# One core, attention and two feed-forward layers: the weight conversions' integer addition moves to VectorE, three attention units take P times V in plain float32, and the norms of phi are made by two operations

## The chip, the core and the metric

The kernel runs on one core of a Trainium2 chip. A core has engines that work side by side, each through its own queue, in order: TensorE (PE in the profile, with PEld for its weight loads), VectorE (DVE), ScalarE (ACT), GpSimd (POOL) and SyncE (SP, which here only issues transfers). The metric is the device time of one execution in microseconds (us).

## The reference, cut to what matters

```
scores = q k^T / 8, causal;  a = softmax(scores)              # B 4, H 8, S 576, D 64
local  = a v
phi(x) = where(x > 0, x, exp(x) - 1) + 1
mem    = (phi(q) M) / (phi(q) . z + 1e-6)
attn   = sigmoid(beta) * mem + (1 - sigmoid(beta)) * local    # as 2304 x 512
h      = attn @ w_in1;  g = s * relu(h)^2 + b;  x = g @ w_out1      # 512 -> 2048 -> 512
h      = x @ w_in2;     g = h * tanh(softplus(h));  out = g @ w_out2
```

The four weight matrices arrive as 64-bit floats, and the kernel makes 32-bit floats of them itself.

## The kernel before

**Stages.** Three run into one another: attention, the first layer (`first`, `y_part`: matmuls at L798 and L871), the second layer (matmuls at L1003 and L1069). Beside the first stage the weights of layer 1 are converted in 32 pieces of 128x512 (`convert(1, ...)`), and beside the last third of layer 1 those of layer 2, in 32 more.

**The order.** Nearly every operation is a step with an engine, an estimated duration and a priority. `Plan.order` plays the steps through and writes each engine's queue in the order that comes out; on the chip each engine then runs its queue in that order, and waits on semaphores. While PE has nothing to do in the first 85 us of that plan, it gets products of zeros (L1239).

**Attention.** A unit is one batch and head. It has five tiles of 128 queries, group TA (tiles 0 to 2) and group TB (tiles 3 and 4). Batch 0 runs as eight TA half-units and then eight TB half-units, called `early`; batches 1 to 3 are 24 whole units. Of a unit: phi of q (L498 on POOL, L499 on ACT, L500 on DVE); the norms phi . z, one 64-wide product with a running sum for each tile, which is an operation and a read of its accumulator (L492), then L496 and L504; the memory columns of P (L555, POOL); scores (L534 for an early unit, L538 and L539 for the others); masked row minimum (L543); exp (L552); scaling of each tile's rows (L569 on POOL or DVE, L567 on ACT, by the letters of `E_NORM` and `F_NORM`); transposes (L596); P times V (L624); copy to `xs` (L632) and out.

In a unit that isn't early the products are split: each operand is a rounded high part and a low rest, both in a faster matmul format. So P's transposes are copied high by ACT (L601) and subtracted to a low part by DVE (L604), V likewise (L646, L647), each matmul of P times V runs once with `PTh` and once with `PTl`, and DVE adds the two halves of the result (L635). An early unit takes P times V in plain float32, without a low part and without L604, L646, L647 and L635.

**A conversion** (`convert`): a transfer brings 512 pairs of words; ACT scales the high word into the new exponent (L695) and rounds the low word to its top three bits (L700); DVE shifts the first by three (L702) and puts the sign in (L703); POOL adds the two as integers (L705); for layer 1 ACT then makes the high part (L712) and DVE the low rest (L715).

Of the kernel before, what the change touches and what calls it, by code (L numbers as in the profile page):

```python
# [9 lines left out]
F32 = mybir.dt.float32  # L10
F32R = mybir.dt.float32r
BF16 = mybir.dt.bfloat16
I32 = mybir.dt.int32
U32 = mybir.dt.uint32
AF = mybir.ActivationFunctionType
ALU = mybir.AluOpType
PSUM = bass.MemoryType.PSUM
DRAM = bass.MemoryType.DRAM

P = 128  # L20
MASKED = -1.0e30
HUGE = 3.0e38
SIGN = -0x80000000
PE, ACT, DVE, POOL, DMA = range(5)


# [8 lines left out]
CONV = (3.0, 3.81, 4.18, 3.12)  # L35
CONV2 = 655.2

E_TRA, E_NORM, E_XS = 'AAAADA', 'PPDDA', 'A'
F_NORM = 'PPDDA'
C_HI, C_W, C2_W = 'AAAA', 'AAAA', 'AAAA'  # L40

PLACE_A = (0, 3, 2, 4)
# [289 lines left out]
def attention_then_two_ffn(ctx: ExitStack, tc: tile.TileContext, qk, qz, vm, beta,  # L332
# [99 lines left out]
    def unit(b, h, prio, groups=(TA, TB), place=None):  # L432
# [5 lines left out]
            attention_steps.append(plan.add(engine, us, prio, f, r, w, keep=keep, share=share))  # L438

        early = place is not None and place < 5  # L440
        first_half = groups == (TA,)
        tiles = [t for g in groups for t in g]
        nb = tiles[-1] + 1
# [44 lines left out]
            return qn()[:, lo_t + 1:lo_t + n_t + 1]  # L488

        def norm_phi():  # L490
            for t in tiles:
                nc.vector.tensor_tensor_reduce(qn()[:, t + 1, :], ex.t[:, t, :], qn()[:, 0, :], 1.0, 0.0,  # L492
                                               ALU.mult, ALU.add, nm.t[:, t:t + 1])

        def norm_gate():
            nc.vector.tensor_scalar(nm.t[:, mine], nm.t[:, mine], 1e-6, igate[:, 0, h:h + 1], op0=ALU.add, op1=ALU.mult)  # L496
# [2 lines left out]
        add(ACT, act_us(n_t * D), lambda: nc.scalar.activation(ex.t[:, mine], ex.t[:, mine], AF.Exp), [ex], [ex])  # L499
        add(DVE, dve_us(n_t * D), lambda: nc.vector.scalar_tensor_tensor(ex.t[:, mine], q_rows(), 0.0, ex.t[:, mine],  # L500
                                                                         op0=ALU.max, op1=ALU.add), [ex, qn_b], [ex])
        add(DVE, 0.22 * n_t, norm_phi, [ex, qn_b], [nm, qn_b])
        add(DVE, 0.13, norm_gate, [nm], [nm])
        add(DVE, 0.09, lambda: nc.vector.reciprocal(nm.t[:, mine], nm.t[:, mine]), [nm], [nm])  # L504

# [75 lines left out]
        def weigh(g):  # L581


            first = {t: 2 * t if t < 3 else 4 * (t - 3) for t in g}
            names = ("PTh", "PTl") if not early else (("PTl",) if h % 2 else ("PTh",))
            PT = [Buf(R[x], [P, 9, P], F32 if early else F32R) for x in names]
            for t in g:
                cuts = (0, t + 1) if t < 4 else (0, 3, 5)
                for c0, c1 in zip(cuts, cuts[1:]):
                    ps = Buf(R["a"], [P, 4, P])  # L590
                    at_ = slice(first[t] + c0, first[t] + c1)
                    n = c1 - c0

                    def mm(ps=ps, t=t, c0=c0, c1=c1):
                        for c in range(c0, c1):
                            nc.tensor.transpose(ps.t[:, c - c0, :], Pt[t].t[:, c * P:(c + 1) * P], ident)  # L596

                    e = on(E_TRA[t + (c0 > 0)]) if early else ACT

                    def high(ps=ps, at_=at_, n=n, dve=e == DVE):  # L600
                        (nc.vector.tensor_copy if dve else nc.scalar.copy)(PT[0].t[:, at_], ps.t[:, :n])  # L601

                    def low(ps=ps, at_=at_, n=n):
                        nc.vector.tensor_tensor(PT[1].t[:, at_], ps.t[:, :n], PT[0].t[:, at_].bitcast(F32), op=ALU.subtract)  # L604

                    add(PE, 0.01 + 0.108 * n, mm, [Pt[t]], [ps], PT)
                    add(e, dve_us(n * P) if e == DVE else act_us(n * P) - 0.04, high, [ps], [PT[0]])
                    if not early:
                        add(DVE, dve_us(n * P), low, [ps, PT[0]], [PT[1]])

            n = len(g) * P
            skip = D if g[0] == 0 else 0
            m = n - skip
            q0 = max(0, g[0] * P - D)
            pv, xs = Buf(R["a"], [P, 512]), Buf(R["xs"], [D, 320])

            def mm():
                for c in range(g[-1] + 1):
                    ts = [t for t in g if t >= c]
                    f = [first[t] + c for t in ts]  # L620
                    cols = slice((ts[0] - g[0]) * P, n)
                    for k, x in enumerate(PT):
                        o, v = (pv.t[:D, cols], vx()[:, c, :]) if early else (pv.t[:, cols], V.t[:, c, :])
                        nc.tensor.matmul(o.rearrange("p (t q) -> p t q", q=P), v,  # L624
                                         x.t[:, f[0]:f[-1] + 1:f[1] - f[0] if len(f) > 1 else 1, :],
                                         start=(c == 0 and k == 0), stop=(c == g[-1] and k == len(PT) - 1))

            cols = 6 if g == TA else 9
            add(PE, cols * P * 0.0017 if early else 0.06 + cols * P * 0.00085, mm, PT + [vx_b if early else V], [pv])
            e = on(E_XS) if early else ACT  # L630
            add(e, dve_us(m) if e == DVE else act_us(m) - 0.04,
                lambda: (nc.vector.tensor_copy if e == DVE else nc.scalar.copy)(xs.t[:, :m], pv.t[:D, skip:n] if early else pv.t[D:, skip:n]),  # L632
                [pv], [xs])
            if not early:
                add(DVE, dve_us(m), lambda: nc.vector.tensor_tensor(xs.t[:, :m], pv.t[:D, skip:n], xs.t[:, :m], op=ALU.add),  # L635
                    [pv, xs], [xs])
            c0, p0 = b * S + q0, h % 2 * D
            add(DMA, 0.5, lambda: nc.sync.dma_start(x_d[p0:p0 + D, h // 2, c0:c0 + m], xs.t[:, :m]), [xs], [x_in[b, groups_all.index(g)]])
# [2 lines left out]
            score(t)  # L641
        norm(groups[0])
        add(DMA, 0.6 * nb / NQ, lambda: nc.sync.dma_start(vx(), vm[b, h][:, :nb]), w=[vx_b])
        if not early:
            V = Buf(R["V"], [P, NQ, 2 * D], F32R)
            add(ACT, act_us(NQ * D), lambda: nc.scalar.copy(V.t[:, :, :D], vx()), [vx_b], [V])  # L646
            add(DVE, dve_us(NQ * D), lambda: nc.vector.tensor_tensor(V.t[:, :, D:], vx(), V.t[:, :, :D].bitcast(F32), op=ALU.subtract),  # L647
                [vx_b, V], [V])
# [25 lines left out]
    def convert(layer, prio, which, r, j, raw, after=()):  # L674


        w_in, w_out = ((w_in1, w_out1), (w_in2, w_out2))[layer - 1]
        fc = r * FPR + j
        src = w_in[j * P:(j + 1) * P, r * 512:(r + 1) * 512] if which == "in" else w_out[fc * P:(fc + 1) * P, :]
        w = Buf(R["w32"], [P, 512], I32)  # L680

        def words():
            return raw.t[:, :1024].rearrange("p (n two) -> p n two", two=2)

        def f32():
            return w.t.bitcast(F32)

        add(DMA, 1.5, prio, lambda: nc.sync.dma_start(words(), src.bitcast(I32).rearrange("p (n two) -> p n two", two=2)),
            w=[raw], after=after).lag = 1.0 if layer == 1 else 3.0

        e = on((C_W if layer == 1 else C2_W)[j])
        add(e, 0.52 if e == ACT else 0.335, prio,
            (lambda: nc.scalar.activation(f32(), words()[:, :, 1].bitcast(F32), AF.Copy, scale=2.0 ** -112)) if e == ACT else  # L695
            (lambda: nc.vector.tensor_scalar(f32(), words()[:, :, 1].bitcast(F32), 2.0 ** -112, None, op0=ALU.mult)),
            [raw], [w])

        low_words = Buf()
        add(ACT, 0.52, prio, lambda: nc.scalar.activation(words()[:, :, 0], words()[:, :, 0].bitcast(U32), AF.Copy,  # L700
                                                          scale=2.0 ** -29), [raw], [low_words])
        add(DVE, 0.335, prio, lambda: nc.vector.tensor_scalar(w.t, w.t, 3, None, op0=ALU.logical_shift_left), [w], [w])  # L702
        add(DVE, 0.6, prio, lambda: nc.vector.scalar_tensor_tensor(w.t, words()[:, :, 1], SIGN, w.t,  # L703
                                                                   op0=ALU.bitwise_and, op1=ALU.bitwise_or), [raw, w], [w])
        add(POOL, 1.23 if layer == 1 else 1.45, prio, lambda: nc.gpsimd.tensor_tensor(w.t, w.t, words()[:, :, 0], op=ALU.add),  # L705
            [raw, low_words, w], [w])
        if layer == 1:
            hi, lo = f"w{which[0]}h", f"w{which[0]}l"
            hi_dve, lo_dve = C_HI[j] == "D", C_LO[j] == "D"
            half = Buf()  # L710
            add(DVE if hi_dve else ACT, 0.335 if hi_dve else 0.52, prio,
                lambda: (nc.vector.tensor_copy if hi_dve else nc.scalar.copy)(w_at(hi, r, j), f32()), [w],  # L712
                [W[hi, r], half])
            add(DVE if lo_dve else POOL, 0.6 if lo_dve else 1.23, prio,
                lambda: (nc.vector if lo_dve else nc.gpsimd).tensor_tensor(w_at(lo, r, j), f32(),  # L715
                                                                           w_at(hi, r, j).bitcast(F32), op=ALU.subtract),
                [w, half], [W[lo, r]])
        return w
# [568 lines left out]
```

## Time and profile before

| | us |
|---|---|
| median of 3 runs (1041.0 to 1042.43) | 1041.44 |
| the profiled execution | 1041.25 |
| its span on the core | 1039.4 |
| PE busy | 1004.7 (97%) |
| DVE busy | 845.4 (81%) |
| ACT busy | 713.2 (69%) |
| POOL busy | 278.2 (27%) |
| mean granted clock of PE, as a share of full speed | 0.991 |

The span is the time from the core's first to its last instruction, and 1.85 us lie outside it. Shares are means over stages with different limits, and matmuls are pipelined, so PE's busy time counts gaps between matmuls that a reader has to find otherwise.

### The profile page before, as it was taken

The numbers are of one execution on the slowest core, as the hardware profiler recorded it, in microseconds if no ns is written. First come the engines' busy times: TensorE is split into PE (matmuls) and PEld (weight loads), VectorE is DVE, ScalarE is ACT, GpSimd is POOL, SyncE is SP. The second block draws the span as 40 slices with busy tenths as digits, with TensorE's granted clock in tenths as the row PEclk, the third lists the DMA queues.
The fourth block names the chain that finished last, engine by engine and source line by source line (L and its number), as shares of the span: only waits on it lengthen the run. The fifth ranks groups of instructions, "written<-read, shape, count | busy, mean of one in ns | idle before, by whom it ended". The sixth has DMA issues, their size and how long they took to land.

```text
span 1039.4 us, 20180 instructions
## 1 busy us (share of the span) xinstructions
PE 1004.7 (97%) x6708; PEld 928.9 (89%) x6708; DVE 845.4 (81%) x2347; ACT 713.2 (69%) x1606; POOL 278.2 (27%) x386
## 2 busy tenths in 40 slices
PE   6889997999999999999999999999999999999998
PEld 4657787999999999999888778899999999999998
DVE  6899899999999989986568896359985789767864
ACT  6876897888988888876777897536753456434552
POOL 6864354333343334320234220000110000100010
PEclk9998998999999999999999999999999999999999
DMA  9663563323432333225888887558686766676464
GB/s 260 181 195 103 152 193 95 111 85 99 137 111 72 93 119 94 83 64 157 234 254 265 271 290 232 213 192 288 214 295 226 233 220 202 238 236 216 151 218 168
DMA packets 88984, 188.63 MB, mean 181 GB/s; under 512 B 8752, under 2 KB 63024, under 8 KB 81584
## 3 DMA queue, kind: packets, MB, share of 16 engines
q1 hardware_dynamic: 81392, 135.95, 42.3%
q0 software_dynamic: 7056, 51.38, 14.7%
q8 instruction: 53, 0.87, 0.3%
q14 instruction: 51, 0.42, 0.1%
q10 hardware_dynamic: 432, 0.01, 0.0%
HBM read 144.32 MB, written 42.99 MB: 180 GB/s over the span
## 4 chain that ended last, share of the span: by engine, by line
PE 59%; DVE 14%; issue 11%; ACT 7%; DMA 4%; POOL 3%; POOLq 0%; DVEq 0%; ACTq 0%; SPq 0%
PE bank L1003 15%; PE bank L1069 12%; PE bank L871 12%; PE bank L798 11%; PE bank L624 3%; PE bank L596 3%; DVE PTl L604 2%; PE bank L538 1%; DVE Pt L543 1%; PE bank L539 1%; DVE stage L703 1%; ACT PTh L601 1%; ACT Pt L552 1%; DVE stage L702 1%; POOL stage L705 1%
## 5 line engine op out<-in xcount | busy, mean ns | idle before, releaser
L1069 PE MATMUL bank<-woh,S 128*128 128x256 f32 x792 | 107.3, 283 | 0.0
L1069 PEld LDWEIGHTS bank<-woh,S 128*128 128x128 f32 x792 | 100.8, 192 | 0.1
L1069 PE MATMUL bank<-wol,S 128*128 128x256 f32 x720 | 98.1, 283 | 0.0
L555 POOL TENSOR_SCALAR Pt<-ex,nm 128x64 f32<-128x64 f32 x148 | 74.5, 516 | 85.1 <-PE bank L596 38.5
L1003 PE MATMUL bank<-wi,woh 128*128 128x384 f32 x426 | 94.0, 335 | 0.0
L552 ACT ACTIVATE Pt<-Pt,mx 128x64 f32<-128x64 f32 (+4 forms) x148 | 81.8, 555 | 16.5 <-DVE mx L543 15.7
L1069 PEld LDWEIGHTS bank<-wol,S 128*128 128x128 f32 x720 | 91.8, 192 | 0.0
L596 PE MATMUL bank<-ident,Pt 128*128 128x128 f32 x432 | 67.0, 281 | 10.8 <-POOL Pt L569 7.9
L1003 PEld LDWEIGHTS bank<-wi,woh 128*128 128x128 f32 x426 | 75.6, 188 | 0.6
L1003 PE MATMUL bank<-wi,wol 128*128 128x384 f32 x294 | 76.0, 335 | 0.1
L705 POOL TENSOR_TENSOR stage<-stage 128x512 int32<-128x512 int32 x36 | 48.5, 1348 | 99.6 <-DVE stage L703 50.0
L604 DVE TENSOR_TENSOR PTl<-bank,PTh 128x128 fp32r<-128x128 f32 (+1 forms) x144 | 63.8, 480 | 2.3 <-ACT PTh L601 1.2
L596 PEld LDWEIGHTS bank<-ident,Pt 128*128 128x128 f32 x432 | 49.7, 143 | 17.0 <-POOL Pt L569 10.3
L569 POOL TENSOR_SCALAR Pt<-Pt,rs 128x64 f32<-128x64 f32 x64 | 45.3, 749 | 70.7 <-DVE rs L574 54.6
L984 POOL DMA_DIRECT2D wol<-wo_split_d x17 | 9.2, 542 | 201.7 <-DVE wi L727 109.9
L543 DVE CUSTOM_DVE_ANT_0 Pt<-bank,mask 128x320 f32<-128x320 f32 (+3 forms) x148 | 59.1, 416 | 3.3 <-PE bank L539 1.6
L601 ACT CAST PTh<-bank 128x128 fp32r<-128x128 f32 (+1 forms) x144 | 54.8, 430 | 2.6 <-PE bank L596 1.7
L871 PE MATMUL bank<-gh,wol 128*128 128x256 f32 x320 | 54.0, 292 | 0.0
L871 PE MATMUL bank<-gl,woh 128*128 128x256 f32 x320 | 53.7, 290 | 0.0
L1003 PEld LDWEIGHTS bank<-wi,wol 128*128 128x128 f32 x294 | 53.0, 188 | 0.6 <-DMA wol<-wi_split_d 0.3
L871 PE MATMUL bank<-gh,woh 128*128 128x256 f32 x320 | 53.1, 289 | 0.0
L798 PE MATMUL bank<-xh,wi 128*128 128x256 f32 x320 | 50.6, 289 | 1.4 <-DVE rt L849 1.3
(278 smaller groups left out, 2961.9 us busy)
## 6 DMA issues: line engine op xcount, KB each, us to landing
wol<-wo_split_d POOLq DMA_DIRECT2D x17, 1024.0 KB, 5.2
woh<-wo_split_d POOLq DMA_DIRECT2D x16, 1024.0 KB, 5.8
qk<-in_qk SPq DMA_DIRECT2D x24, 608.0 KB, 3.9
stage<-in_w_out SPq DMA_DIRECT2D x23, 512.0 KB, 4.5
wo_split_d<-high SPq DMA_DIRECT2D x44, 256.0 KB, 3.1
stage<-in_w_in SPq DMA_DIRECT2D x21, 512.0 KB, 4.8
stage<-wi_d SPq DMA_DIRECT2D x24, 384.0 KB, 5.3
wi_split_d<-woh SPq DMA_DIRECT2D x8, 1024.0 KB, 4.9
```

The lines of the kernel that those rows point to most:

```text
L543: nc.vector.tensor_tensor_reduce(Pt[t].t[:, D + lo:D + hi], ps.t[:, :hi - lo], mask[:, SP - w + lo:SP - w + hi], -SCALE, mx.t[:, t:t + 1] ...
L552: nc.scalar.activation(Pt[t].t[:, D:w + D], Pt[t].t[:, D:w + D], AF.Exp, bias=mx.t[:, t + i:t + i + 1], scale=-1.0, accum_out=rs.t[:, t:t ...
L555: add(POOL, 0.3, lambda: nc.gpsimd.tensor_scalar(Pt[t].t[:, :D], ex.t[:, t, :], nm.t[:, t:t + 1], 1.0, op0=ALU.mult, op1=ALU.mult), [ex, n ...
L569: (nc.vector if e == DVE else nc.gpsimd).tensor_scalar(x, x, r, None, op0=ALU.mult)
L596: nc.tensor.transpose(ps.t[:, c - c0, :], Pt[t].t[:, c * P:(c + 1) * P], ident)
L601: (nc.vector.tensor_copy if dve else nc.scalar.copy)(PT[0].t[:, at_], ps.t[:, :n])
L604: nc.vector.tensor_tensor(PT[1].t[:, at_], ps.t[:, :n], PT[0].t[:, at_].bitcast(F32), op=ALU.subtract)
L705: add(POOL, 1.23 if layer == 1 else 1.45, prio, lambda: nc.gpsimd.tensor_tensor(w.t, w.t, words()[:, :, 0], op=ALU.add), [raw, low_words, ...
L798: nc.tensor.matmul(ph, w_at(nm, r, cc)[:, o:o + P], x_at(x, cc), start=(part == 0 and cc == 0), stop=(part == 2 and cc == NCC - 1))
L871: nc.tensor.matmul(acc[ec // per].t[:, (ec % per) * n:(ec % per + 1) * n], w_at(nm, r, jj)[:, ec * P:(ec + 1) * P], t(x), start=(big and f ...
L1003: nc.tensor.matmul(ps.t[:, :H2], w[i // 4].t[:, j, kk, i % 4], x[kk].t[:, k], start=begin and part == kk == 0, stop=part == 2 and kk == 1, ...
L1069: nc.tensor.matmul(acc[t].t[:, :DH], s.t[:, j, t * P:(t + 1) * P], x.t[:, k, q % 4], start=q == part == 0, stop=q == NQ2 - 1 and part == 2)
```

## The change

**The conversions.** DVE's operation that put the sign in (128x512 int32) becomes a bit operation on 16-bit halves: the sign bit of the high word goes into the upper half of the low word. DVE then adds the two as integers; the program issues it as one instruction on 1024 16-bit halves. POOL has no part in a conversion any more. The sign's step now waits for ACT's rounding of the low word (L700), since it writes beside it.

**Early units.** Tile 2's rows are scaled by POOL, not by DVE (`E_NORM`), in the eight TA half-units.

**Plain.** The first three units of batch 1 take P times V as early units do (`PLAIN`).

**Norms of phi.** One product over all tiles of the unit, with z broadcast, and one sum over the last axis.

```diff
-E_TRA, E_NORM, E_XS = 'AAAADA', 'PPDDA', 'A'
+E_TRA, E_NORM, E_XS = 'AAAADA', 'PPPDA', 'A'
 F_NORM = 'PPDDA'
+PLAIN = 3
...
         early = place is not None and place < 5
+        plain = early or (b == 1 and h < PLAIN)
...
         def norm_phi():
-            for t in tiles:
-                nc.vector.tensor_tensor_reduce(qn()[:, t + 1, :], ex.t[:, t, :], qn()[:, 0, :], 1.0, 0.0,
-                                               ALU.mult, ALU.add, nm.t[:, t:t + 1])
+            nc.vector.tensor_tensor(q_rows(), ex.t[:, mine], qn()[:, 0:1, :].to_broadcast([P, n_t, D]), op=ALU.mult)
+            nc.vector.tensor_reduce(nm.t[:, mine], q_rows(), axis=AXIS, op=ALU.add)
...
-            names = ("PTh", "PTl") if not early else (("PTl",) if h % 2 else ("PTh",))
-            PT = [Buf(R[x], [P, 9, P], F32 if early else F32R) for x in names]
+            names = ("PTh", "PTl") if not plain else ("PTl" if (h % 2 if early else g == TB) else "PTh",)
+            PT = [Buf(R[x], [P, 9, P], F32 if plain else F32R) for x in names]
...
-                    if not early:
+                    if not plain:
                         add(DVE, dve_us(n * P), low, [ps, PT[0]], [PT[1]])
...
+        def limbs():
+            return raw.t[:, :1024].bitcast(U16).rearrange("p (n four) -> p n four", four=4)
...
-        add(DVE, 0.6, prio, lambda: nc.vector.scalar_tensor_tensor(w.t, words()[:, :, 1], SIGN, w.t,
-                                                                   op0=ALU.bitwise_and, op1=ALU.bitwise_or), [raw, w], [w])
-        add(POOL, 1.23 if layer == 1 else 1.45, prio, lambda: nc.gpsimd.tensor_tensor(w.t, w.t, words()[:, :, 0], op=ALU.add),
-            [raw, low_words, w], [w])
+        signed = Buf()
+        add(DVE, 0.335, prio, lambda: nc.vector.tensor_scalar(limbs()[:, :, 1], limbs()[:, :, 3], 0x8000, None, op0=ALU.bitwise_and),
+            [raw, low_words], [signed])
+        add(DVE, 0.75, prio, lambda: nc.vector.tensor_tensor(w.t, w.t, words()[:, :, 0], op=ALU.add), [raw, signed, w], [w])
```

In the other places of `weigh` and at V's split, `early` becomes `plain` in the same way, and the estimates that `Plan` takes for the changed steps change with them. Line numbers of the changed kernel are two to five higher (L702 becomes L707, L703's place is L709, L705's is L711, L492 becomes L494 and L495, L569 becomes L571, L624 becomes L626).

The plan writes all queues anew. POOL's queue from its first memory columns (L555) on, before: `Pt_0`, `Pt_1` and `B` hold tiles of P.

```order
L555 TENSOR_SCALAR Pt_0_158<-ex_139,nm_149 128x64
L555 TENSOR_SCALAR Pt_0_162<-ex_139,nm_149 128x64
L555 TENSOR_SCALAR Pt_0_174<-ex_139,nm_149 128x64
L498 TENSOR_SCALAR ex_182<-wol_0_134 128x192
L705 TENSOR_TENSOR stage<-stage 128x512
L498 TENSOR_SCALAR ex_209<-woh_0_141 128x192
L569 TENSOR_SCALAR Pt_0_158<-Pt_0_158,rs_160 128x64
L569 TENSOR_SCALAR Pt_0_162<-Pt_0_162,rs_160 128x192
L555 TENSOR_SCALAR Pt_1_215<-ex_182,nm_199 128x64
```

And now:

```order
L557 TENSOR_SCALAR Pt_0_155<-ex_139,nm_149 128x64
L557 TENSOR_SCALAR Pt_0_161<-ex_139,nm_149 128x64
L557 TENSOR_SCALAR Pt_0_170<-ex_139,nm_149 128x64
L500 TENSOR_SCALAR ex_178<-wol_0_134 128x192
L500 TENSOR_SCALAR ex_208<-woh_0_141 128x192
L571 TENSOR_SCALAR Pt_0_155<-Pt_0_155,rs_157 128x64
L571 TENSOR_SCALAR Pt_0_161<-Pt_0_161,rs_157 128x192
L571 TENSOR_SCALAR Pt_0_170<-Pt_0_170,rs_157 128x320
L557 TENSOR_SCALAR Pt_1_215<-ex_178,nm_204 128x64
```

The integer addition is gone from between the units, and a third scaling, 320 wide, has come into each.

DVE's queue at the first conversion, before (`ISA` at L543 is the row minimum and the read of its accumulator, `stage` holds the piece):

```order
L702 TENSOR_SCALAR stage<-stage 128x512
L543 ISA Pt_0_162,mx_159<-bank_111,mask 128x192
L543 ISA mx_159 128x1
L703 SCALAR_TENSOR_TENSOR stage<-stage 128x512
L543 ISA Pt_0_174,mx_159<-bank_112,mask 128x320
L543 ISA mx_159 128x1
L500 SCALAR_TENSOR_TENSOR ex_182<-wol_0_134,ex_182 128x192
```

And now:

```order
L707 TENSOR_SCALAR stage<-stage 128x512
L545 ISA Pt_0_161,mx_156<-bank_111,mask 128x192
L545 ISA mx_156 128x1
L709 TENSOR_SCALAR stage<-stage 128x512
L545 ISA Pt_0_170,mx_156<-bank_112,mask 128x320
L545 ISA mx_156 128x1
L711 ISA stage<-stage 128x1024
```

The sign's operation is a different one in the same place, and the addition, `ISA` on 1024 halves, stands behind it in the same queue.

PE's queue at the first whole unit's P times V, group TA, before (`V` holds V's two parts, the L798 and L871 rows are layer 1):

```order
L871 MATMUL bank_109<-gl_1660,woh_0_1325 128x256 x2
L624 MATMUL bank_113<-PTh_1798,V_1771 128x384
L624 MATMUL bank_113<-PTl_1799,V_1771 128x384
L624 MATMUL bank_113<-PTh_1798,V_1771 128x256
L624 MATMUL bank_113<-PTl_1799,V_1771 128x256
L624 MATMUL bank_113<-PTh_1798,V_1771 128x128
L624 MATMUL bank_113<-PTl_1799,V_1771 128x128
L798 MATMUL bank_106<-xh_890,wih_0_1549 128x256 x4
```

And now (`vx` is V as it was loaded):

```order
L876 MATMUL bank_109<-gh_1748,wol_0_1346 128x256 x2
L626 MATMUL bank_112<-PTh_1889,vx_1777 64x384
L626 MATMUL bank_112<-PTh_1889,vx_1777 64x256
L626 MATMUL bank_112<-PTh_1889,vx_1777 64x128
L598 MATMUL bank_113<-ident,Pt_0_1797 128x128 x4
L598 MATMUL bank_111<-ident,Pt_0_1803 128x128 x3
```

Three plain float32 matmuls stand for six split ones, and the transposes of TB follow them at once. Each plain one shows as two records in a trace.

## Rows read from the trace of the kernel before

**Rows 1.** Windows view: length, busy us and count (PE, PEld, DVE, ACT, POOL), clock, DMA.

```profile
25.00:50.00 25.00, 21.49 (x122) 15.01 (x121) 21.24 (x85) 20.69 (x62) 22.17 (x31) 1.00 0.70 195
...
60.00:200.00 140.00, 126.81 (x824) 106.85 (x823) 130.05 (x398) 110.95 (x263) 59.99 (x74) 0.95 0.47 143
200.00:475.00 275.00, 271.34 (x2165) 263.34 (x2166) 254.63 (x974) 224.00 (x596) 97.29 (x161) 1.00 0.31 93
475.00:650.00 175.00, 172.81 (x843) 145.53 (x843) 132.59 (x249) 138.15 (x264) 45.77 (x32) 0.99 0.82 252
```

**Rows 2.** Chain that ended last, 60 to 200: start, us, what.

```profile
70.23 1.67 DVE stage L703
...
92.29 1.68 DVE wil L715
...
123.40 1.20 DVE rs L572
```

**Rows 3.** Timeline: first and last DVE instruction held beside a POOL addition.

```profile
10.06 1.29 POOL L705 TENSOR_TENSOR stage<-stage 128x512 int32<-128x512 int32 x1 [0.48 <-ACT Pt L552]
...
10.25 1.32 DVE L500 SCALAR_TENSOR_TENSOR ex<-wol,ex 128x192 f32<-128x192 f32 x1
...
29.38 0.34 DVE L500 SCALAR_TENSOR_TENSOR ex<-wih,ex 128x192 f32<-128x192 f32 x1
...
615.62 1.80 DVE L853 TENSOR_TENSOR xh<-g,xh 128x512 fp32r<-128x512 f32 x1
```

**Rows 4.** Windows view of L705 alone (POOL busy us and count, clock, DMA).

```profile
60.00:200.00 140.00, 28.93 (x22) 0.95 0.47 143
```

**Rows 5.** Groups, conversions and norms: count, busy us, mean ns, idle before.

```profile
L703 DVE SCALAR_TENSOR_TENSOR low<-stage,low 128x512 int32<-128x512 int32 x8 | 5.5, 690 | 0.2
L705 POOL TENSOR_TENSOR stage<-stage 128x512 int32<-128x512 int32 x36 | 48.5, 1348 | 99.6 <-DVE stage L703 50.0 <-ACT xs L632 8.6 <-ACT stage L700 5.3
L727 DVE TENSOR_TENSOR woh<-stage,woh 128x1024 fp32r<-128x1024 f32 x14 | 17.1, 1218 | 4.0 <-ACT woh L726 4.0
L492 DVE CUSTOM_DVE_ANT_0 qn<-ex,qn 128x64 f32<-128x64 f32 x136 | 25.5, 241 | 0.6
L492 DVE DVE_READ_ACCUMULATOR2_ANT nm<- 128x1 f32 x160 | 12.4, 78 | 0.0
```

**Rows 6.** Timeline: the shift of a conversion, undisturbed.

```profile
563.01 0.42 DVE L702 TENSOR_SCALAR stage<-stage 128x512 int32<-128x512 int32 x1
```

**Rows 7.** Groups of DVE work that a plain unit leaves out.

```profile
L604 DVE TENSOR_TENSOR PTl<-bank,PTh 128x128 fp32r<-128x128 f32 (+1 forms) x144 | 63.8, 480 | 2.3 <-ACT PTh L601 1.2
L635 DVE TENSOR_TENSOR xs<-bank,xs 64x320 f32<-64x320 f32 (+1 forms) x48 | 21.4, 445 | 4.6 <-ACT xs L632 3.9
L647 DVE TENSOR_TENSOR V<-vx,V 128x320 fp32r<-128x320 f32 x24 | 12.0, 498 | 0.3 <-ACT V L646 0.2
```

**Rows 8.** Timeline: plain TA, then a split TA's first and last matmul.

```profile
34.15 1.51 PE L624 MATMUL bank<-PTl,vx 128*64 128x384 f32 x6
155.32 0.34 PE L624 MATMUL bank<-PTh,V 128*128 128x384 f32 x1
...
156.17 0.28 PE L624 MATMUL bank<-PTl,V 128*128 128x128 f32 x1
```

**Rows 9.** Chain: a plain TB's P times V, an early unit's scores, a split TB.

```profile
112.52 2.09 PE bank L624 x10
...
117.19 2.68 PE bank L534 x8
...
164.96 1.15 PE bank L624 x10
```

**Rows 10.** POOL's group of the 320-wide shape; timeline of POOL and DVE without an addition.

```profile
L498 POOL TENSOR_SCALAR ex<-qn 128x320 f32<-128x320 f32 x24 | 26.2, 1092 | 45.0 <-DMA qn<-in_qz 41.2 <-DVE Pt L569 3.9
...
52.07 3.52 POOL L569 TENSOR_SCALAR Pt<-Pt,rs 128x64 f32<-128x64 f32 x4
...
53.65 0.38 DVE L569 TENSOR_SCALAR B<-B,rs 128x320 f32<-128x320 f32 x1
```

More of the change, by code (lines that the diff above doesn't have):

```diff
@@ L14 @@
 U32 = mybir.dt.uint32
+U16 = mybir.dt.uint16
 AF = mybir.ActivationFunctionType
 ALU = mybir.AluOpType
+AXIS = mybir.AxisListType.X
 PSUM = bass.MemoryType.PSUM
@@ L22 @@
 HUGE = 3.0e38
-SIGN = -0x80000000
 PE, ACT, DVE, POOL, DMA = range(5)
@@ L501, in unit @@
                                                                          op0=ALU.max, op1=ALU.add), [ex, qn_b], [ex])
-        add(DVE, 0.22 * n_t, norm_phi, [ex, qn_b], [nm, qn_b])
+        add(DVE, 2 * dve_us(n_t * D), norm_phi, [ex, qn_b], [nm, qn_b])
         add(DVE, 0.13, norm_gate, [nm], [nm])
@@ L596, in mm @@
                             nc.tensor.transpose(ps.t[:, c - c0, :], Pt[t].t[:, c * P:(c + 1) * P], ident)
-                    e = on(E_TRA[t + (c0 > 0)]) if early else ACT
+                    e = on(E_TRA[t + (c0 > 0)]) if plain else ACT
                     def high(ps=ps, at_=at_, n=n, dve=e == DVE):
@@ L622, in mm @@
                     for k, x in enumerate(PT):
-                        o, v = (pv.t[:D, cols], vx()[:, c, :]) if early else (pv.t[:, cols], V.t[:, c, :])
+                        o, v = (pv.t[:D, cols], vx()[:, c, :]) if plain else (pv.t[:, cols], V.t[:, c, :])
                         nc.tensor.matmul(o.rearrange("p (t q) -> p t q", q=P), v,
@@ L628, in weigh @@
             cols = 6 if g == TA else 9
-            add(PE, cols * P * 0.0017 if early else 0.06 + cols * P * 0.00085, mm, PT + [vx_b if early else V], [pv])
-            e = on(E_XS) if early else ACT
+            add(PE, cols * P * 0.0017 if plain else 0.06 + cols * P * 0.00085, mm, PT + [vx_b if plain else V], [pv], share=0.5 if plain else 1.0)
+            e = on(E_XS) if plain else ACT
             add(e, dve_us(m) if e == DVE else act_us(m) - 0.04,
-                lambda: (nc.vector.tensor_copy if e == DVE else nc.scalar.copy)(xs.t[:, :m], pv.t[:D, skip:n] if early else pv.t[D:, skip:n]),
+                lambda: (nc.vector.tensor_copy if e == DVE else nc.scalar.copy)(xs.t[:, :m], pv.t[:D, skip:n] if plain else pv.t[D:, skip:n]),
                 [pv], [xs])
-            if not early:
+            if not plain:
                 add(DVE, dve_us(m), lambda: nc.vector.tensor_tensor(xs.t[:, :m], pv.t[:D, skip:n], xs.t[:, :m], op=ALU.add),
@@ L643, in unit @@
         add(DMA, 0.6 * nb / NQ, lambda: nc.sync.dma_start(vx(), vm[b, h][:, :nb]), w=[vx_b])
-        if not early:
+        if not plain:
             V = Buf(R["V"], [P, NQ, 2 * D], F32R)
```

## The prediction

> **What bounds the kernel now.** I read the windows view first, since the shares of the page mix stages. From 200 on PE is the limit: 2165 matmul records in 275 us, 7.87 in a microsecond, while DVE is busy for 93% beside it; from 475 to 650 PE is idle for only 2.2 us of 175; and the rest to the end has no stall of PE that is worth a row. Between 60 and 200 it is different: 824 records in 140 us, 5.9 in a microsecond, with DVE busy for 130.05 us (93%) and a granted clock of 0.95 [rows 1]. PE's own need there: 824 records at 7.87 are 105 us. The eight TB half-units take P times V in plain float32, 2.09 us where a split one takes 1.15, so 8 x 0.94 = 7.5 us more; their scores, 48 such records, take 2.68 us for eight where the steady rate gives 1.02, so 10 us more [rows 1, 9]. That makes 122 us, and about 18 us of PE are lost between 60 and 200. [...]
>
> The chain of waits says on what. It runs through DVE instructions far longer than their kind: 1.67 us for the sign, 1.68 for a low rest, 1.20 for a 3-wide operation [rows 2]. Beside each of them POOL adds integers. So I went through DVE's timeline beside all 64 additions and took, for each DVE instruction, what it lasts beyond the lower fifth of its form. Beside 52 of the 64 one lasts clearly longer (over 0.06 us); the first and the last are shown, and the first has 0.34 us without an addition beside it [rows 3]. The excess is 24.5 us beside the first 32 additions, of which 17 us fall between 60 and 200 (22 additions [rows 4]), and 19.3 us beside the 32 of layer 2.
>
> Before 60 the stage of the TA half-units is POOL's: 22.17 of 25 us between 25 and 50 [rows 1].
>
> **Conversions.** A piece loses 1.35 us on POOL [rows 5]. On DVE the sign's 0.69 goes [rows 5], and a bit operation with one input and the integer addition come. For the first the nearest rows are the shift, the same shape with one input, 0.42, and the sign itself, 0.69 [rows 5, 6]; I take 0.42. The trace has no addition on halves: one 512-wide operation with two inputs takes 0.69, a 1024-wide one 1.22 [rows 5]. The instruction has 1024 halves, but 512 words; I take 0.69 and keep 1.22 for the range. So DVE pays 0.42 + 0.69 - 0.69 = 0.42 a piece (at worst 1.22), 9.2 us for 22 pieces, and gets back the 17 us for which the additions held it. The new wait on the rounding of the low word (L700) blocks DVE's queue if ACT is late; ACT makes it right behind L695, for which DVE waits already, so I cost it at nothing: the shift and, in the first piece, a row minimum stand between. If that cover goes, what stands behind it is the next unit's row minimum, and exp on ACT waits for that.
>
> **Plain units.** DVE leaves out six subtractions, 63.8 / 24 = 2.66 us, V's rest, 0.50, and the sum of the halves, 21.4 / 24 = 0.89 [rows 7]: 4.05 a unit, 12.1 in all, all of it before 200, where the split P times V of those three units now begin at 155 and later [rows 8]. PE pays: plain TA 1.51 us against 155.32 to 156.45, 1.13; plain TB 2.09 against 1.15 [rows 8, 9]. That is 0.38 + 0.94 = 1.3 a unit, 4 us.
>
> **Norms.** Five products with their reads are 5 x (0.241 + 0.078) = 1.6 us [rows 5]. In their place stand a product and a sum over 320 elements. No sum over an axis is in the trace; I take the 320-wide two-input 0.50 [rows 7] for both, so 0.6 less for a whole unit, for some five of them before 200: 3 us. If the sum took twice as much, 0.1 would be left. A TA half-unit saves 0.3 (three products, 0.96, against two of the 0.34 of a 192-wide one [rows 3]), a TB one nothing. After 200 the 19 units save 11 us of DVE, which I cost at nothing: PE is full there.
>
> **Tile 2.** Eight scalings leave DVE, 0.38 each, and cost POOL about 1.1, by its other one-input operation of this shape [rows 10]: 8.8 us, against the 10 x 1.35 = 13.5 that it loses before 60. POOL is relieved by 5 us, but each tile 2 comes 0.7 later to its transposes. I take 2 us of gain before 60, with bounds of 5 us either way.
>
> [...] Beside four scalings on POOL, 3.52 us in a row, DVE's own scaling takes 0.38 as ever [rows 10]. [...]
>
> **The sum.** Between 60 and 200 DVE gets 17 - 9.2 + 12.1 + 3 = 23 us less work, from 130 to 107, and PE 4 more, 126. Then PE needs more than DVE, and the 18 us lost are the most that can come back. Some will stay: weights arrive in chains of six steps, and ACT is at 79%. I take two thirds, 12, less the 4: 8 us. Before 60: 2. From 475 to 650 DVE gets 19.3 back and pays 32 x 0.42 = 13.4; PE was idle for 2.2 there: 1. In all 11: 1041.25 - 11 = **1030 us**. The profiled execution lies 0.2 under the median, so this holds for the median too.
>
> **Rivals.**
>
> *The first stage grows.* The eight scalings hold DVE for 24.5 / 31 = 0.8 each, 6 us, in the stage that POOL sets, instead of giving back 2. What speaks for it: tile 2 is the last and the longest of a half-unit. Against: rows 10. 1030 + 8 = 1038.
>
> *The addition is slow.* At 1.22, and 0.69 for the sign, DVE pays 0.8 more a piece, 18 us between 60 and 200, and is relieved by 5 us only. With 2 or 3 of PE's loss back after the 4, and nothing more after 475: 1038.
>
> *PE is the limit already (slower).* If the 18 us are order and clock rather than waits for DVE, the relief buys nothing and the three plain units are paid in full: 1041 + 4 = 1045. It decides if, between 145 and 200, PE's rate stays under 6.5 records a microsecond although DVE has idle time. [...] Against: DVE's 93% and the chain through the held instructions.
>
> *More comes back.* All 18 return, POOL's 5 before 60 and 4 from 475 on: 1041 - 18 + 4 - 5 - 4 = 1018.
>
> **Chances.** Forecast 0.55; first stage 0.12; slow addition 0.13; PE 0.10; more 0.10. The range from 1018 to 1043 takes in all but the slower case and the outer ends. The forecast alone spans 1024 to 1035. A measurement of this kernel tells 0.2%, 2.1 us, from no change. Half of the two small-gain rivals falls within that or beside it: faster 0.78, same 0.12, slower 0.10.
>
> **What would show it.** Right, if no DVE instruction lasts a microsecond beyond its form before 200; if the sign is near 0.42 and the addition near 0.7; if the plain P times V take 1.5 and 2.1 us; if DVE is under 110 us in what were 140; and if the last conversion and the end of the first 824 records come some 8 us earlier. Wrong, if DVE is held beside the scalings, if the addition takes 1.2, or if DVE is idle and PE's clock is low between 145 and 200.

## The result, and the profile after

The changed kernel takes 1028.78 us (median of 4 runs, 1027.99 to 1030.37), the kernel before beside it 1041.22 (4 runs, 1039.37 to 1042.43): a ratio of 0.9877, 95% interval [0.986, 0.9893]. That is 12.4 us less, where 11 were forecast. Each ratio in this text is to the kernel before, run beside it. The profiled execution took 1030.37 us, its span is 1028.6, against 1039.4 before.

The windows view after, columns and stretches as in [rows 1]:

```profile
25.00:50.00 25.00, 22.66 (x132) 16.01 (x130) 23.10 (x72) 21.14 (x58) 21.97 (x27) 1.00 0.74 209
...
60.00:200.00 140.00, 137.36 (x918) 114.02 (x917) 129.01 (x386) 117.93 (x286) 39.08 (x66) 1.00 0.51 150
200.00:475.00 275.00, 272.89 (x2172) 264.28 (x2171) 250.41 (x787) 221.18 (x581) 92.86 (x151) 1.00 0.33 99
475.00:650.00 175.00, 174.96 (x824) 146.06 (x824) 134.88 (x277) 140.83 (x265) 0.00 (x0) 1.00 0.83 265
```

Between 60 and 200 PE makes 918 records instead of 824, at a clock of 1.00 instead of 0.95. DVE is as busy as before, 129 us, but with more work done. From 25 to 50 POOL is still busy for 21.97 of 25 us, although the additions are gone; it was the fullest engine there before (22.17), and now DVE (23.10) and PE (22.66) are fuller.

The groups view after, for the operations that came (count, busy us, mean ns, idle before), answering to [rows 5, 10]:

```profile
L709 DVE TENSOR_SCALAR stage<-stage 128x512 uint16<-128x512 uint16 x44 | 33.1, 759 | 2.6 <-ACT stage L705 2.3
L711 DVE CUSTOM_DVE_ANT_0 stage<-stage 128x1024 uint16<-128x1024 uint16 x36 | 24.7, 687 | 0.4
L495 DVE TENSOR_REDUCE nm<-qn 128x5 f32<-128x320 f32 x24 | 11.7, 488 | 0.8
L494 DVE TENSOR_TENSOR qn<-ex,qn 128x320 f32<-128x320 f32 x24 | 11.6, 484 | 0.2
L571 POOL TENSOR_SCALAR Pt<-Pt,rs 128x320 f32<-128x320 f32 x4 | 6.0, 1489 | 0.0
L571 POOL TENSOR_SCALAR B<-B,rs 128x320 f32<-128x320 f32 x4 | 5.8, 1455 | 0.0
```

The addition (L711) takes 0.69 and both parts of the norms 0.49, as estimated. The sign (L709) takes 0.76 where 0.42 was taken, outside even the bound of 0.69. The eight scalings of tile 2 on POOL (the last two rows) take 11.8 us instead of 8.8. DVE's timeline after shows a conversion with nothing held:

```profile
121.29 0.41 DVE L707 TENSOR_SCALAR stage<-stage 128x512 int32<-128x512 int32 x1
121.62 0.74 DVE L709 TENSOR_SCALAR stage<-stage 128x512 uint16<-128x512 uint16 x1
122.16 0.32 DVE L494 TENSOR_TENSOR qn<-ex,qn 128x128 f32<-128x128 f32 x1
122.51 0.29 DVE L495 TENSOR_REDUCE nm<-qn 128x2 f32<-128x128 f32 x1
122.71 0.68 DVE L711 CUSTOM_DVE_ANT_0 stage<-stage 128x1024 uint16<-128x1024 uint16 x1
```

The excess of DVE's instructions was 24.5 us beside POOL's additions before 200; counted in the same way beside all that POOL still does there, it is about 3. In layer 2 it falls from 19.3 to nothing, since POOL has no work left there.

The first stage did not get shorter. The chain that ended last, at the end of that stage:

```profile
55.02 3.67 POOL Pt L571 x3
59.17 1.44 PE bank L626 x6
...
62.57 1.44 PE bank L626 x6
```

Three scalings in a row on POOL stand ahead of the last two of the early TAs' P times V. The last one starts at 62.5 us where it started at 59.0 before.

To compare stages I worked out from all matmul records what TensorE loses: the time from one record's start to the next one's, less the lower quartile of that time for records of the same line and form (a shorter time counts as negative); products of zeros count in full. What is not lost I call useful work. Each row is one profiled execution, up to 6 us off its kernel's median, so a difference of a few us in one cell is only a sign. In us, by stretch of the span:

| kernel | 0–50 | 50–100 | 100–150 | 150–200 | 200–500 | 500–650 | 650–end | lost | useful |
|---|---|---|---|---|---|---|---|---|---|
| before | 23.0 | 18.5 | 6.0 | 12.4 | 20.1 | 5.8 | 1.2 | 87.0 | 941.8 |
| after | 24.9 | 14.2 | 3.7 | 3.9 | 19.7 | 1.5 | 4.4 | 72.2 | 945.8 |

So 15 us come back between 50 and 200 and 4 in layer 2's conversions. Part of both is the clock. The kernel before had three stretches at a granted clock of 0.50, called the lower clock below:

```profile
95.70:102.50 6.80, 6.80 (x26) 5.29 (x25) 6.28 (x21) 4.35 (x10) 1.89 (x3) 0.50 0.44 127
174.20:181.00 6.80, 5.38 (x23) 4.98 (x24) 6.01 (x22) 3.04 (x7) 3.29 (x4) 0.50 0.15 32
580.40:583.80 3.40, 3.38 (x8) 2.70 (x9) 3.40 (x7) 3.40 (x8) 0.00 (x0) 0.50 0.86 210
```

Of what PE lost, 3.2, 4.0 and 1.7 us lie in them, so 7.2 of the 36.9 between 50 and 200. The changed kernel has no such stretch before 764 us. On the other side 1.9 are lost anew before 50, 3 after 650, and 4 are the plain units' dearer matmuls. The loss after 650 is mostly a new wait and, right behind it, a stretch at the lower clock (0.50 from 764.8 us, 3.4 long), in which 1.5 are lost; the waits view after, 740 to 780 (us, times, longest):

```profile
PE bank L1074 <- DMA woh<-wo_split_d: 1.8, 1, 1.8
```

### The profile page after: what moved, and what is told of

It is laid out like the page before. It is cut to its first block, busy times and chain, and to the rows that moved or that the text cites. A ratio compares the mean times of both kernels' runs of the same rounds, so it can differ in the third digit from the quotient of the medians.

```text
span 1028.6 us, 19915 instructions
## 1 busy us (share of the span) xinstructions
PE 1007.6 (98%) x6751; PEld 930.3 (90%) x6751; DVE 837.4 (81%) x2139; ACT 712.7 (69%) x1600; POOL 204.7 (20%) x330
## 3 DMA queue, kind: packets, MB, share of 16 engines
q0 software_dynamic: 7056, 51.38, 14.9%
## 4 chain that ended last, share of the span: by engine, by line
PE 71%; DVE 11%; issue 8%; ACT 4%; DMA 3%; POOL 2%; POOLq 0%; SPq 0%; DVEq 0%; ACTq 0%
PE bank L803 15%; PE bank L1008 15%; PE bank L876 15%; PE bank L1074 14%; PE bank L626 4%; PE bank L598 3%; PE bank L536 2%; POOL Pt L571 2%; DVE PTl L606 2%; PE bank L540 1%; DVE gl L859 1%; DVE Pt L545 1%; PE bank L541 1%; ACT Pt L554 1%; DMA woh<-wo_split_d 1%
## 5 line engine op out<-in xcount | busy, mean ns | idle before, releaser
L571 POOL TENSOR_SCALAR Pt<-Pt,rs 128x64 f32<-128x64 f32 (+2 forms) x68 | 52.5, 808 | 88.8 <-DVE rs L576 72.8
L545 DVE CUSTOM_DVE_ANT_0 Pt<-bank,mask 128x320 f32<-128x320 f32 (+3 forms) x148 | 59.6, 419 | 8.5 <-PE bank L536 3.7
L606 DVE TENSOR_TENSOR PTl<-bank,PTh 128x384 fp32r<-128x384 f32 (+1 forms) x126 | 55.8, 480 | 1.8 <-ACT PTh L603 1.7
L876 PE MATMUL bank<-gh,woh 128*128 128x256 f32 x320 | 52.2, 285 | 0.0
L603 ACT CAST PTh<-bank 128x384 fp32r<-128x384 f32 (+2 forms) x126 | 47.1, 431 | 3.4 <-PE bank L598 2.8
L848 ACT ACTIVATE rt<-bank,sb 128x256 f32<-128x256 f32 x80 | 37.9, 474 | 14.9 <-PE bank L803 13.6
```

The lines of the kernel that those rows point to most:

```text
L545: nc.vector.tensor_tensor_reduce(Pt[t].t[:, D + lo:D + hi], ps.t[:, :hi - lo], mask[:, SP - w + lo:SP - w + hi], -SCALE, mx.t[:, t:t + 1] ...
L571: (nc.vector if e == DVE else nc.gpsimd).tensor_scalar(x, x, r, None, op0=ALU.mult)
L876: nc.tensor.matmul(acc[ec // per].t[:, (ec % per) * n:(ec % per + 1) * n], w_at(nm, r, jj)[:, ec * P:(ec + 1) * P], t(x), start=(big and f ...
```

## The experiments

The theory was that the additions' leaving POOL makes the gain, because DVE was held at moments that mattered. The rivals: DVE's total load counts, the plan's new order made the gain, or the other three edits did. One more comes with the same edit: a piece is ready earlier, and POOL's queue is free for the units. The additions put back on POOL, below, separate that from the holds only in layer 2. The same table for the kernels that follow:

| kernel | 0–50 | 50–100 | 100–150 | 150–200 | 200–500 | 500–650 | 650–end | lost | useful |
|---|---|---|---|---|---|---|---|---|---|
| conversions alone | 23.0 | 13.1 | 3.0 | 14.1 | 17.4 | 1.5 | 2.4 | 74.4 | 941.4 |
| conversions undone | 26.8 | 24.4 | 5.8 | 7.2 | 18.5 | 2.5 | 6.5 | 91.8 | 945.6 |
| no plain units | 27.8 | 16.6 | 3.8 | 8.3 | 16.7 | 0.9 | 1.7 | 75.8 | 942.0 |
| old norms | 26.1 | 14.0 | 3.5 | 4.2 | 14.9 | 0.5 | 1.7 | 64.9 | 946.0 |
| tile 2 on DVE | 22.2 | 10.7 | 4.3 | 6.2 | 17.2 | 4.7 | 1.5 | 66.8 | 947.7 |
| two-input operations added | 28.0 | 22.9 | 5.3 | 7.3 | 20.3 | 14.0 | 2.7 | 100.6 | 945.0 |
| one-input operations added | 27.8 | 26.2 | 4.3 | 6.2 | 20.8 | 6.8 | 1.0 | 93.2 | 946.6 |
| new norms, old price | 25.8 | 14.8 | 3.5 | 3.0 | 15.1 | 0.5 | 0.7 | 63.3 | 946.9 |
| old norms, new price | 25.8 | 14.0 | 3.2 | 3.7 | 18.0 | 0.4 | 2.4 | 67.5 | 945.9 |

**The conversions alone.** The kernel before with this only:

```diff
-        add(DVE, 0.6, prio, lambda: nc.vector.scalar_tensor_tensor(w.t, words()[:, :, 1], SIGN, w.t, ...
-        add(POOL, 1.23 if layer == 1 else 1.45, prio, lambda: nc.gpsimd.tensor_tensor(w.t, w.t, words()[:, :, 0], op=ALU.add), ...
+        add(DVE, 0.335, prio, lambda: nc.vector.tensor_scalar(limbs()[:, :, 1], limbs()[:, :, 3], 0x8000, ...
+        add(DVE, 0.75, prio, lambda: nc.vector.tensor_tensor(w.t, w.t, words()[:, :, 0], op=ALU.add), ...
```

> The kernel before with the conversions' part alone: sign by a 16-bit operation and integer addition on VectorE; no plain units beyond the five early ones, old norms, tile 2 as before. Theory (VectorE was held beside GpSimd's additions, and the holds stood on the path, so it counts when an instruction is late and not only how much work there is): most of the gain is here, 1031 to 1035 us, and the excess beside GpSimd's operations falls from 24.5 us to about 2 in the first 200 us. Rival (it is VectorE's total load that counts): the new pair of operations takes 0.76 us a piece more than the sign alone did, 22 x 0.76 = 17 us between 60 and 200, which is what the holds cost, 17 us; so nothing comes back: 1039 to 1044 us. Second rival (the order alone): anything within 3 us of 1041.

Measured: 1024.17 us against 1043.68, ratio 0.9821 [0.98, 0.9842]. That is more than either theory gave, and more than the whole change. The load theory falls: DVE is busy for 130.80 us between 60 and 200, where before it was 130.05, and yet 8 us of PE came back between 50 and 150 and 4 in layer 2. The excess beside POOL's work before 200 is 2.9 us. Between 150 and 200 nothing came back.

**The conversions undone**, the same lines the other way round in the changed kernel.

> The changed kernel with the conversions as before (sign on 32-bit words, integer addition on GpSimd); plain units, norms and tile 2 as changed. Theory (holds): 1035 to 1039 us, since the holds are back and only the relief of VectorE by the plain units (12 us) and the norms (3 us) less TensorE's 4 stays. Rival (load): the same load on VectorE as in the changed kernel between 60 and 200, so about its time, 1028 to 1032 us, plus about 1 us from the second layer's conversions.

Measured: 1043.31, ratio 1.0007 [0.9991, 1.0022]. The other three edits together give nothing. In the table they gain 5 us from 150 to 200 and pay them back: 10 before 100, where POOL has the additions and tile 2 as well, 5 after 650, and 4 in useful work. The profiled execution took 1049.52 us, 6 above the median, so the table makes these larger than they mostly are. The holds theory (1035 to 1039) was off, the load theory (1028 to 1032) far off.

**No plain units** (`PLAIN = 0` in the changed kernel).

> The changed kernel without the three plain units. VectorE gets 12 us of work back between 60 and 200 and TensorE loses 4 us. Load: 1028.8 + 12 - 4 = 1037 us. Holds: VectorE has room once it is not held, so less of the 12 shows: 1029 to 1032 us. If TensorE alone sets the stretch: 1028.8 - 4 = 1025 us.

Measured: 1028.36 against 1043.68, ratio 0.9845 [0.9814, 0.9876]; the interval touches the changed kernel's, so no difference is shown. The load theory's 12 us more did not come; the ratio is that of 1025 us in the first comparison, what was expected if TensorE alone sets the stretch. The windows view of this kernel, 150 to 200, where the plain units would stand, and beside it the changed kernel's:

```profile
150.00:200.00 50.00, 44.34 (x354) 42.70 (x353) 48.55 (x148) 41.01 (x107) 17.11 (x27) 1.00 0.38 114
```

```profile
150.00:200.00 50.00, 49.54 (x356) 43.37 (x355) 45.22 (x141) 41.10 (x110) 17.28 (x32) 1.00 0.39 115
```

The relief of DVE is real, 48.55 to 45.22 us, and PE loses 4.4 us less there. The dearer matmuls take 3.8 (945.8 less 942.0).

**Old norms** (the old five products, at their old price in the plan).

> The changed kernel with the norms of phi as before, one product with a sum for each tile. VectorE gets 0.6 us back for each whole unit, 3 us between 60 and 200 and 11 us after it. Load: 1028.8 + 3 = 1032 us. Holds, or TensorE full after 200: 1029 to 1030 us. Order alone: within 3 us either way.

Measured: 1023.68, ratio 0.9806 [0.9791, 0.982]: 7 us faster than with the new norms, which no theory had. In the table the gain lies from 200 on: 4.8 us between 200 and 500, 1.0 to 650, 2.7 after it.

**Tile 2 on DVE** (`E_NORM` back to `PPDDA`).

> The changed kernel with the scaling of tile 2 on VectorE again. In the changed kernel the eighth early P times V starts at 62.5 us, in the kernel before at 59.0, with the conversions alone changed at 57.3. If the scaling on GpSimd is what made the first stage later, the eighth starts at 58 us or before and the time is 4 to 5 us under the changed kernel's, a ratio to before near 0.983. If the order of the plan did it, the eighth stays at 61 to 65 us and the ratio is 0.986 to 0.990.

Measured: 1023.13 against 1041.45, ratio 0.9823 [0.9796, 0.985]. The end of the first stage in PE's timeline:

```profile
55.58 0.44 PE L598 MATMUL bank<-ident,Pt 128*128 128x128 f32 x2 [0.81 <-POOL Pt L571]
...
56.89 1.51 PE L626 MATMUL bank<-PTl,vx 128*64 128x384 f32 x6
```

The eighth P times V starts at 56.9 us instead of 62.5, and PE loses 6.2 us less before 100. PE's waits for POOL's scalings before 60 us come to 1.8 us instead of 3.1. So with the additions gone POOL was relieved, and tile 2 took the relief away again.

**The new norms' operations and their order, apart.** First the old operations in the new order:

```diff
         def norm_phi():
-            nc.vector.tensor_tensor(q_rows(), ex.t[:, mine], qn()[:, 0:1, :].to_broadcast([P, n_t, D]), op=ALU.mult)
-            nc.vector.tensor_reduce(nm.t[:, mine], q_rows(), axis=AXIS, op=ALU.add)
+            for t in tiles:
+                nc.vector.tensor_tensor_reduce(...)
...
         add(DVE, 2 * dve_us(n_t * D), norm_phi, [ex, qn_b], [nm, qn_b])
```

> The changed kernel with the old operations for the norms of phi (five products with a sum each), but in the changed kernel's order of work. With the old operations and their own order the ratio to before was 0.9806, against 0.9877 of the changed kernel. If the two new operations themselves cost the 7 us, this gives about 0.981. If it is the order, this gives 0.987 to 0.990; by VectorE's load it would be 3 us slower than the changed kernel, 0.990.

Then the new operations at the old price (`0.22 * n_t`, 1.10 us for a whole unit, where the changed kernel's plan has 2 x 0.40):

> The changed kernel with the new operations for the norms of phi, planned at the old price (0.22 us a tile), so in the order that the old ones had with that price. Ratios to before so far: new operations in their order 0.9877, old in their order 0.9806, old in the order of the new 0.9845. If the order makes the difference, this is 0.980 to 0.982; if the operations do, 0.984 to 0.988; if each makes half, 0.983 to 0.985.

Measured: 0.9845 [0.9818, 0.9872] and 0.9834 [0.9812, 0.9857]. The second lies clear of the changed kernel's 0.9877: with the same operations, the order alone costs 4 us. In the table these four lose 15 us between 200 and 500 with the old price, and 18 to 20 with the new. That is not a mark of the price, though: the kernel without plain units, at the new price, loses 16.7 there, and the kernel before, at the old one, 20.1. Which step of the new order costs is not shown. Whether the operations themselves cost the rest stays open: 0.9845 against 0.9877 and 0.9806 against 0.9834 point to 3 us, but in both pairs the intervals overlap, and the second pair's stretches don't differ where norms are made.

**An addition put back on POOL, with nothing waiting for it.** In the changed kernel, planned as it was:

```diff
+        def joined():
+            nc.vector.tensor_tensor(w.t, w.t, words()[:, :, 0], op=ALU.add)
+            nc.gpsimd.tensor_tensor(words()[:, :, 1], words()[:, :, 1], words()[:, :, 0], op=ALU.add)
-        add(DVE, 0.75, prio, lambda: nc.vector.tensor_tensor(w.t, w.t, words()[:, :, 0], op=ALU.add), [raw, signed, w], [w])
+        add(DVE, 0.75, prio, joined, [raw, signed, w], [w])
```

> The changed kernel, in its own order, with one more integer addition on GpSimd behind each of the 64 additions on VectorE, into words that nobody needs any more; the buffer of a piece is free 1.5 us later. Nothing waits for its result. Theory (holds): VectorE is held beside it again, an excess of 15 to 25 us in the first 200 us, and the time goes up by 8 to 14 us, a ratio to before of 0.995 to 1.001. Rival (load and order): VectorE and TensorE have the same work in the same order, so 0.987 to 0.990.

And with `tensor_scalar_min(words()[:, :, 1], words()[:, :, 1], 0.0)` on POOL in its place:

> The same as the run with the additional integer additions, with an operation of one input on GpSimd in their place, on the same words. Theory (the hold needs two inputs from GpSimd): VectorE is held for less than 5 us in the first 200 us, and the ratio stays within 0.987 to 0.991; if it is GpSimd's load and the later free buffer that cost, it is as slow as the run with the additions.

Measured: 1058.63, ratio 1.016 [1.0131, 1.0188], and 1051.03, ratio 1.0085 [1.006, 1.011]: 30 us and 22 us worse than the changed kernel, far more than expected. The second expectation also fails in kind: the one-input operation was to hold DVE for less than 5 us before 200 and holds it for about 10. DVE's and POOL's timeline, first with the two-input operation (L713), then with the one-input operation:

```profile
560.36 1.55 POOL L713 TENSOR_TENSOR stage<-stage 128x512 int32<-128x512 int32 x1 [3.09 <-DVE stage L709]
560.93 1.27 DVE L707 TENSOR_SCALAR stage<-stage 128x512 int32<-128x512 int32 x1
...
562.94 1.55 POOL L713 TENSOR_TENSOR raw<-raw 128x512 int32<-128x512 int32 x1 [1.03 <-DVE raw L709]
563.50 1.53 DVE L862 TENSOR_TENSOR xl<-g,xl 128x512 fp32r<-128x512 f32 x1
```

```profile
561.44 1.67 POOL L713 TENSOR_SCALAR raw<-raw 128x512 f32<-128x512 f32 x1
561.61 1.13 DVE L862 TENSOR_TENSOR xl<-g,xl 128x512 fp32r<-128x512 f32 x1
...
562.66 0.41 DVE L750 TENSOR_TENSOR sc<-stage 128x256 f32<-128x256 f32 x1
```

A shift that takes 0.42 lasts 1.27, and a low rest of 0.69 lasts 1.53. Behind the one-input operation, which itself lasts longer, the same rest lasts 1.13. Over the 64 pieces the two-input operation holds DVE for 41.5 us and the one-input operation for 22.4. In layer 2 POOL does nothing else, and there the run with the longer hold loses more, although POOL is busy for less: PE loses 14.0 us from 500 to 650 where, from 475 to 650, DVE is held for 25.3 and POOL busy for 52.2, and 6.8 where DVE is held for 12.7 and POOL busy for 66.2; 1.5 in the changed kernel, with neither. But the loss is no price for each microsecond held. In the same stretch the kernel before is held for 19.3 and loses 5.8, "conversions undone" is held for 18.6 and loses 2.5, and "tile 2 on DVE" is not held and loses 4.7. Of these losses 1.6 to 2.4 us lie in a stretch at the lower clock, but for the changed kernel and "conversions undone", which have none there.

Before 100 it is the other way: 50.9 lost with the two-input operations, 54.0 with the longer ones that hold less, 39.1 without. Two things are seen there and not told apart. The clock fell: from 0 to 100 it is 0.95 and 0.86, and of the losses 5.7 and 13.5 us lie in stretches at the lower clock. The windows view with the one-input operations, and after:

```profile
0.00:100.00 100.00, 81.85 (x378) 58.46 (x379) 73.86 (x220) 64.60 (x171) 71.26 (x91) 0.86 0.59 168
```

```profile
0.00:100.00 100.00, 87.61 (x488) 65.40 (x489) 84.57 (x267) 77.80 (x200) 54.37 (x78) 1.00 0.68 192
```

And what stands behind an added operation in POOL's queue, the scalings above all, comes later. The wait for the scalings, on PE, before 60 us, with the two-input and with the one-input operations:

```profile
PE bank L598 <- POOL Pt L571: 5.4, 5, 2.5
```

```profile
PE bank L598 <- POOL Pt L571: 6.4, 4, 2.5
```

It is 3.1 us in the changed kernel. Both runs also keep a piece's buffer longer, and what that costs isn't told apart.

**The conversions of layer 2 alone** (the new lines if `layer == 2`, in the kernel before).

> The kernel before with the new conversions in layer 2 alone, where the additions are GpSimd's only work and the other engines' order is hardly touched. Theory (holds): TensorE loses 6 us between 500 and 650 in the kernel before and 1.5 us with the additions on VectorE, so the time is 3 to 5 us less, a ratio of 0.995 to 0.997, and VectorE is held by nothing there. Rival (load): VectorE gets 19.3 us of holds back and pays 24 us, so no gain, 0.999 to 1.002.

Measured: 1037.78 against 1042.23, ratio 0.996 [0.9942, 0.9978], 4.2 us, as the holds gave. PE loses 1.3 us from 500 to 650, where before lost 5.8, 1.7 of them in the stretch at the lower clock; up to 500 the two lose the same (79.7 and 80.0). The windows view, 550 to 600, of this kernel and of the kernel before:

```profile
550.00:600.00 50.00, 49.84 (x219) 40.71 (x218) 46.62 (x103) 46.16 (x93) 0.00 (x0) 1.00 0.96 320
```

```profile
550.00:600.00 50.00, 48.30 (x203) 38.88 (x202) 42.89 (x79) 40.55 (x80) 17.25 (x12) 0.97 0.88 269
```

DVE is busier (46.62 against 42.89) and PE makes 219 records instead of 203: load rose, and the loss went. The addition's 1.3 us on POOL left the piece's own path as well; that the hold counts beside it rests on the added operations above.

**Versions that keep what paid.** Conversions and plain units, without the other two:

> The changed kernel with only the conversions and the three plain units; tile 2 and the norms of phi as in the kernel before. If what tile 2 (0.0054) and the norms (0.0071) cost adds up, the ratio to before is 0.9877 - 0.0054 - 0.0071 = 0.975, about 1016 us, and the eighth early P times V starts at 58 us or before. If each of them only shifts the order and the best orders are reached by either alone, it stays at 0.980 to 0.984.

Measured: 1023.86, ratio 0.9825 [0.9802, 0.9849]: the savings don't add up. The same with the sign by the old form:

```diff
+        add(DVE, 0.6, prio, lambda: nc.vector.scalar_tensor_tensor(w.t, words()[:, :, 1], SIGN, w.t,
+                                                                   op0=ALU.bitwise_and, op1=ALU.bitwise_or), [raw, w], [w])
+        add(DVE, 0.75, prio, lambda: nc.vector.tensor_tensor(w.t, w.t, words()[:, :, 0], op=ALU.add), [raw, low_words, w], [w])
```

> The run with conversions and plain units alone, with the sign by the 32-bit operation of two inputs of the kernel before (0.69 us) in place of the 16-bit one of one input (0.756); the integer addition stays on VectorE. If the price of the sign operation matters, VectorE gets 0.07 x 64 = 4 us back, of which 22 x 0.07 = 1.5 between 60 and 200, and the time is 1 to 2 us less. The sign no longer waits for the rounding of the low word; if that wait costs, 2 to 4 us less. If neither counts, the same time within 2 us.

Measured: 1025.8, ratio 0.9847 [0.9824, 0.987]. Neither the price of the sign nor its wait shows. The lowest ratio of all is that of the changed kernel with the old norms, 0.9806. With it, five versions with the new conversions lie between 0.9806 and 0.9834, with intervals that touch.

## Why the prediction was right, and where it was not

The forecast of 11 us was met by 12.4, and the bounds held. The place was right too: the additions held DVE between 60 and 200, and most of PE's time came back there once they had left POOL. But the terms were off in both directions and gave most of the gain to the wrong edits, so that the total fits so well is partly luck.

**60 to 200: 12 of PE's 18 us back, less 4.** Measured from 50 to 200: 15.1 back (36.9 lost before, 21.8 after), and 4.0 of useful work more, as the plain units were priced. The clock is at 1.00 instead of 0.95; the 7.2 us that PE lost at the lower clock are part of what came back. So the term was too small by 3.

**Why they came back.** The step that failed is "DVE gets 17 - 9.2 + 12.1 + 3 = 23 us less work": by it 8 us are due to the conversions and 15 to the other edits. The sign took 0.76 instead of 0.42, so the pieces cost DVE 0.69 + 0.76 - 0.69 = 0.76 each and 22 of them 16.7 us: all that the holds had cost. By load the conversions would have given nothing. Alone they gave 0.9821, and the others without them 1.0007. As I read it, the held instructions delayed what stood behind them on DVE at moments when someone waited, while the same 16.7 us spent on operations that the plan had placed were not lost by PE. Layer 2 alone shows most plainly that load is not the measure, and with the added operations the longer hold there went with the larger loss (25.3 us held and 14.0 lost, against 12.7 and 6.8). How much of layer 1's gain is the holds, and how much the new order, POOL's free queue or the clock, is not shown.

**Plain units.** Both sides were sized right: 4 us for PE, and the relief between 150 and 200, where PE lost 12.4 us before, 14.1 with the conversions alone and 9.8 with the plain units besides (of these 4.0, 3.3 and 1.6 at the lower clock). They cancel: 0.9821 without the plain units, 0.9825 with them.

**Norms.** The prices were right (0.97 a unit), the sign of the term was not: the planned price of 0.80 changed the order of the whole units after 200, a stretch that I had costed at nothing because PE is full there. PE's loss there is 20 us of 300, and orders differ in it by 5 and more.

**Tile 2 and the rival "the first stage grows".** The term (2 us of gain before 60) failed; the stage became later, by 3.5 us, and tile 2 on DVE takes 5.6 back. The rival had the place right, the mechanism not: DVE is held by 1.3 us beside all 24 scalings before 60, not by 6. POOL itself is the late one: there the eight scalings take 1.08 to 1.75 us each, where DVE took 0.38.

**475 to 650.** 1 us was forecast, 4.3 came (from 500 on): again the load (19.3 back, now 24 paid) was the wrong measure. But 1.7 of it is the clock, and "conversions undone" loses only 2.5 there with the holds, so 4 is not a sure price of them.

**The other rivals.** The slow addition: 0.69, not 1.22. PE the limit: 356 records from 150 to 200, 7.1 in a microsecond, with DVE at 45.2, so no. More comes back: it did, in the table, and the first stage, the wait after 650 and the norms' order took it.

**The signs named.** Counted again, DVE is held beside 51 of the 64 additions, not 52. The last conversion (L720) starts at 163.8 us instead of 177.4, 13.6 earlier where 8 were expected, and DVE's busy time in those 140 us stayed at 129, not under 110, since PE was given more to feed on.

## What to carry to other kernels

A hold on an engine is not to be netted against new load on it: here equal load in place of the holds was 1.8% faster. So price the two apart, and try the part with the hold by itself. Where a planner orders the work, a new price for a step is a change of its own; run the old operation at the new price and the new one at the old price before crediting the operation. And an engine that a change relieves should not be given the next piece of work in the same step, when its stage is the one that it sets: here tile 2 on POOL cost 5.6 us.

## What the runs showed of the hardware

Of DVE's instructions that overlapped one of these operations on POOL, those that read a matmul's result, row minima (L543, L545) above all, were never stretched: 0 of 26 in the kernel before, 0 of 27 with the two-input operations added, and 0 of 40 with the one-input ones. Shifts were, in 13 of 17, 12 of 21 and 18 of 34. The expectation of the one-input run had drawn POOL's side too narrowly: a one-input operation on POOL, with words eight bytes apart, held DVE as well (22.4 us over 64 of them), while the 24 scalings before 60 in the changed kernel, with one input too, stretched its instructions by 1.3 us in all.

How long they were held differs. Beside the two-input operations, in the kernel before and with them added, no DVE instruction that was stretched by more than 0.2 us ended before POOL's operation did (0 of 109). Beside the one-input ones 45 of 56 did, as the one above: it ended at 562.74, POOL's at 563.11. So in these runs the instructions stretched by more than 0.2 us lasted at least to the end of POOL's operation where it had two inputs, and mostly not where it had one, as far as spans on POOL can be trusted.

The sign's operation takes 0.76 us for 512 halves that stand eight bytes apart, the shift 0.42 for 512 words side by side. Whether the step or the width of the halves makes the difference is not shown. The integer addition, issued on 1024 halves, takes 0.69 us, as long as the old sign, a 512-wide operation with two inputs.
